# A convolution and feed-forward kernel: block products summed on VectorE, one-pass gates, separate tiles for block 1, and dummy matmuls in the opening

## Chip, cores and metric

The kernel runs on one core of one Trainium2 chip. The metric is the device time of one execution in microseconds; "before" is the kernel without the change. TensorE multiplies matrices into PSUM, VectorE and ScalarE do the element work, GpSimd (POOL) does small operations and issues one of the two busy DMA queues, SyncE (SP) issues the other.

## The reference

Four layers act on one sequence of 2048 tokens and 576 channels: a gated long convolution, a feed-forward layer, and both once more with the same weights. Cut to what matters:

```python
def _A_ref(q, k, v, shift_k, ssm_k, ssm_D):
    k_shift = sum over t in 0..3 of k_pad[:, t:t + S, :] * shift_k[:, 3 - t]   # a causal filter of 4 taps
    kv = k_shift * v
    y = irfft2(rfft2(kv padded to 2 S) * rfft2(ssm_k padded to 2 S))[:S]       # causal convolution, per channel
    y = y + kv * ssm_D
    return q * y

def _B_ref(x, w_gate, w_up, w_down):
    return (_gelu(x @ w_gate) * (x @ w_up)) @ w_down                           # 576 -> 4608 -> 576

x = A_q
x = x + _A_ref(_layernorm(x), A_k, A_v, A_shift_k, A_ssm_k, A_ssm_D)
x = x + _B_ref(_layernorm(x), B_w_gate, B_w_up, B_w_down)
x = x + _A_ref(_layernorm(x), ...)
x = x + _B_ref(_layernorm(x), ...)
```

The convolution y does not depend on x, so it is computed once and used in both A layers.

## The kernel before, in words

**Units and visits.** The tokens are cut into four chunks of 512. A unit is one feed-forward layer on one chunk, with the gate and the layernorm ahead of it; there are eight, in the order (0,0), (0,1), (1,0), (1,1), (0,2), (0,3), (1,2), (1,3) of (layer, chunk). The 4608 hidden channels are cut into three phases. A visit is one phase of one unit: twelve groups of 18 matmuls for gate and up (`gu`, L835, two halves of 64 rows side by side), a gelu on ScalarE (L1290) and a product on VectorE (L1291) for each group, and then 96 matmuls down (`down`, L1302) whose sums VectorE adds to `x_c` (L1336; L1331 in the last phase of the first layer, which also gives the sum of each row; L1322 into `ob` for the output). Units run in passes [0], [1,2], [3,4], [5,6], [7], phase by phase, so that there are 24 visits. I count them from the first.

**The convolution** (class `Conv`) works on blocks of 512 tokens, which are the chunks. For block m, `step(m)` makes queues of work: the causal filter and product on VectorE (`kv_ops`, L250, L255, L260); forward transforms of the filter's tokens `ht` and of kv on TensorE (`fwd_eo`, L281), copied out by ScalarE (L284) and crossed by VectorE (`cross`, L289, 16 operations a set), spilled to DRAM (Hd, Kd) by POOL (L336) and read again (`load`, L394, L398); products of block a with filter block m-a for each of four frequency tiles `kt` and two parts (`prod`, L298 to L302, into a bf16 tile `sum`); their addition over a by matmuls with the identity into PSUM (`accumulate`, L308), copied out by ScalarE (L491) or combined by VectorE (`both`, L316); the shift of the last block's result (`shifted`, L321); and the inverse transform on TensorE (`inverse`, L331), copied to `y` by ScalarE (L333). Blocks 1 to 3 run this way beside the visits; block 0 is in the opening.

**What sets the order.** Instructions run in program order on each engine. `Pace` keeps one estimated time for TensorE, VectorE and ScalarE, from the costs at the file's head (C_GU and so on), and `fill` puts work of the convolution and of the next unit's preparation between the groups and the down matmuls when its estimated inputs are due: `conv.run_v` for VectorE, `run_vq` for gates and norms, `run_aq` for ScalarE, `run_p` for TensorE. POOL's small operations, spills and output stores (L339) wait in `conv.spills` until due. The estimates only set the order; semaphores set the times.

**Gates and norms.** Each of 28 row tiles behind the opening gets `(x + nm) * y` (L733) and `t * rstd + x` (L740) on VectorE, the second with the sum of each row. POOL makes the negative mean (L697), ScalarE the sum of squares (L705), POOL `rstd` (L712, L713), VectorE the normed tile `xn` (L762, and a copy L764), and SP two DMA transposes into `xnT` (L792).

**The opening.** A small planner (`Plan`) lists tasks with costs and dependencies and writes out a static order: sine tables, the four taps, kv of block 0 with sums by identity matmuls (L1007), the filter turned by matmuls (L1035), the forward transforms of filter and kv (L272), products, pair sums and differences (L1097), inverses (L1110), the gates (L1144, L1155), norms, transposes (L1196), and the first three groups in two halves (`gu_half`). Block 1's filter tokens go into the one `v` buffer (tag "v"), so v of block 1 is loaded only after their transform.

Of the kernel before, what the change touches and what calls it, by code (L numbers as in the profile page):

```python
# [18 lines left out]
P = 128  # L19
# [4 lines left out]
HW = 288  # L24
# [9 lines left out]
N_KC, N_SM = 4, 6  # L34
C_TT, C_ST, C_BN, C_NORM, C_HT, C_GELU, C_EVA, C_EVD = 0.76, 0.82, 0.47, 0.62, 0.69, 0.6, 0.66, 0.76
# [33 lines left out]
class Plan:  # L69


    LAG = 0.12
# [57 lines left out]
class Conv:  # L130
# [9 lines left out]
    def __init__(self, tc, ctx, pace, A_k, A_v, A_shift_k, A_ssm_k, A_ssm_D, ident, cps, ypool):  # L140
# [15 lines left out]
        self.smp = pool("c_sm", N_SM)  # L156
# [16 lines left out]
        self.ps_free = 0.0  # L173
        self.pr_free = [0.0] * N_SM
# [3 lines left out]
        self.npr = self.nkr = self.nhr = 0  # L178
# [7 lines left out]
    def ps(self):  # L186
        return self.cps()
# [47 lines left out]
    def load_ht(self, b, eng):  # L235
        h = self.kvp.tile([P, RT, self.D], BF16, tag="v", name="ht")
        eng.dma_start(out=h[:], in_=self.hs[b].rearrange("(p i) d -> p i d", i=RT))
        self.ht[b] = h

    def kv_ops(self, b):  # L240
# [4 lines left out]
        def mult(i0, j, dst):  # L245
            def run():
                if j >= KS - 2:
# [6 lines left out]
        def add():  # L254
            nc.vector.tensor_tensor(out=st["acc"][:], in0=st["acc"][:], in1=st["tmp"][:], op=ALU.add)  # L255

        def fin(i0):
            def run():
                v = self.vt_[b]
                nc.vector.tensor_tensor(out=v[:, i0:i0 + 2, :], in0=st["acc"][:], in1=v[:, i0:i0 + 2, :], op=ALU.mult)  # L260
            return run
        for i0 in range(0, RT, 2):
            ops.append(("k", mult(i0, KS - 1, "acc")))
            for j in range(KS - 2, -1, -1):
                ops += [("k", mult(i0, j, "tmp")), ("k", add)]
            ops.append(("v", fin(i0)))
        return ops

    def fwd_full(self, ps, src, kt, s):
        for i in range(RT):  # L270
            for h in range(2):
                self.nc.tensor.matmul(ps[:, h, 0:HW], lhsT=self.fw(kt, s, i),  # L272
                                      rhs=src[:, i, h * HW:(h + 1) * HW], start=(i == 0), stop=(i == RT - 1))

    def fwd_eo(self, src, kt, s, h, scale=1.0):
# [3 lines left out]
        for e in range(2):  # L279
            for i in (e, e + 2):  # L280
                nc.tensor.matmul(ps[:, e, 0:HW], lhsT=self.fw(kt, s, i),  # L281
                                 rhs=src[:, i, h * HW:(h + 1) * HW], start=(i == e), stop=(i == e + 2))
# [8 lines left out]
    def prod(self, part, K, H, dst=None):  # L291
        nc = self.nc
        pr = self.prp.tile([P, 2, self.D], BF16, tag="prod", name="prod")
        if dst is None:
            dst = self.smp.tile([P, self.D], BF16, tag="sum", name="sum")[:]
            self.npr += 1
# [8 lines left out]
    def accumulate(self, ps, pr, first, last):  # L305
        nc = self.nc
        for h in range(2):
            nc.tensor.matmul(ps[:, h, 0:HW], lhsT=self.ident[:], rhs=pr[:, h * HW:(h + 1) * HW],  # L308
                             start=first, stop=last)

    def both(self, kt, part, first, second):

        b = {}
        for sg, op in ((0, ALU.add), (1, ALU.subtract)):
            b[sg] = self.ybp.tile([P, self.D], BF16, tag="yb", name="yb")
            self.nc.vector.tensor_tensor(out=self.halves(b[sg][:]), in0=first, in1=second, op=op)  # L316
# [28 lines left out]
    def step(self, m, kv=None, loaded=False):  # L345
# [21 lines left out]
        if loaded:  # L367
            at["k"] = at["h"] = 0.0
# [3 lines left out]
        self.L.append((lambda: self.hf_at.get(m, NEVER), lv))  # L372
# [1018 lines left out]
```

## Time and profile before

| what | us |
|---|---|
| median of 3 runs (lowest, highest) | 994.07 (993.47, 995.79) |
| the profiled execution | 996.55 |
| its span, first to last instruction | 994.8 |
| mean granted TensorE clock | 0.982 of full speed |

In a profile line, a group of instructions stands as line, engine, operation, output <- input, shape and count, then busy time, mean ns of one, and the idle time of the engine ahead of them with what ended it. PE is TensorE's matmuls and PEld its weight loads, DVE is VectorE, ACT is ScalarE, and SPq and POOLq are the DMA queues' issues. A line of stretches gives the bounds, the length, and for each engine the busy time and count; the three last numbers are TensorE's granted clock, the share of the DMA engines and GB/s. A line of waits gives who waited for whom, the total, how often, and the longest. A line of the time order gives start, length, engine, operation and, in brackets, the idle time ahead and its releaser.

### The profile page before, as it was taken

How to read it: one execution, taken by the hardware profiler on the slowest of the kernel's cores; microseconds unless marked ns; L12 is line 12 of the kernel's file. 1: busy time of each engine (PE TensorE's matmuls, PEld its weight loads, DVE VectorE, ACT ScalarE, POOL GpSimd, SP SyncE). 2: the span in 40 equal slices, each digit the busy share in tenths (PEclk: the TensorE clock that was granted, in tenths of full speed). 3: DMA queues.
4: the chain of work that ended last, by engine and by line, in shares of the span. 5: the costliest groups of instructions: out<-in, count | busy, mean ns of one | idle time of the engine just before them, and what ended most of it. 6: DMA issues, size and time to landing. Idle time of an engine off the chain costs nothing.

```text
span 994.8 us, 19408 instructions
## 1 busy us (share of the span) xinstructions
PE 957.0 (96%) x8282; PEld 551.7 (55%) x8282; DVE 547.0 (55%) x1011; ACT 299.6 (30%) x542; POOL 144.1 (14%) x308
## 2 busy tenths in 40 slices
PE   8799999599999999979999999989999999999998
PEld 5555465346646546545565565555664565466455
DVE  7756787666767565648564664465333324623322
ACT  5543412441322325304212412233112112411211
POOL 3313100512111103222010300131000000200000
PEclk9889999799999999989999999999999999999999
DMA  9979887535943721783391570374271270298730
GB/s 233 278 203 240 196 251 144 119 85 171 192 163 103 142 72 37 133 273 72 97 231 44 127 170 22 66 144 98 50 148 41 48 167 1 48 239 147 165 84 25
DMA packets 129577, 131.03 MB, mean 132 GB/s; under 512 B 43985, under 2 KB 121681, under 8 KB 129490
## 3 DMA queue, kind: packets, MB, share of 16 engines
q1 hardware_dynamic: 119554, 93.34, 43.6%
q0 software_dynamic: 9200, 35.54, 11.0%
q8 instruction: 65, 1.06, 0.5%
q10 hardware_dynamic: 736, 0.90, 0.4%
q14 instruction: 22, 0.18, 0.1%
HBM read 108.53 MB, written 11.80 MB: 121 GB/s over the span
## 4 chain that ended last, share of the span: by engine, by line
PE 89%; DVE 3%; DMA 3%; issue 2%; POOL 1%; ACT 1%; SPq 0%; POOLq 0%; DVEq 0%; ACTq 0%
PE gu L835 55%; PE dn L1302 25%; PE cps L281 2%; PE cps L308 2%; PE ps L272 2%; DMA Hd<-hh 1%; PE cps L331 1%; PE ps L835 1%; DMA wgu<-in_B_w_up_dram 1%; DMA out_dram<-ob 1%; PE ps L1007 1%; POOL rstd L713 0%; DVE hh L289 0%; DVE g_t L733 0%; DVE x_c L740 0%
## 5 line engine op out<-in xcount | busy, mean ns | idle before, releaser
L835 PE MATMUL gu<-xnT,wgu 64*128 64x512 bf16 x5130 | 568.5, 379 | 16.1 <-DVE ob L1322 6.6
L835 PEld LDWEIGHTS <-wgu 64*128 64x128 bf16 x5238 | 257.3, 95 | 328.0 <-issue 39.5
L1291 DVE TENSOR_TENSOR hT<-ga,gu 128x512 bf16<-128x512 f32 x285 | 195.8, 687 | 295.3 <-ACT ga L1290 294.3
L1290 ACT ACTIVATE ga<-gu 128x512 f32<-128x512 f32 x285 | 170.2, 597 | 575.8 <-PE gu L835 574.5
L1302 PE MATMUL dn<-wd,hT 128*128 128x288 bf16 x2304 | 299.2, 286 | 0.5 <-DVE ob L1311 0.5
L1302 PEld LDWEIGHTS <-hT 128*128 128x128 bf16 x2304 | 223.5, 98 | 66.1 <-issue 10.5
L1336 DVE TENSOR_TENSOR x_c<-x_c,dn 128x576 f32<-128x576 f32 x64 | 48.2, 753 | 62.8 <-PE dn L1302 62.2
L697 POOL TENSOR_SCALAR nm<-s 128x1 f32<-128x1 f32 x56 | 20.8, 372 | 337.1 <-DVE x_c L1331 249.8
L705 ACT ACTIVATE junk<-x_c,nm 128x576 bf16<-128x576 f32 x44 | 33.8, 768 | 18.4 <-POOL nm L697 18.4
L284 ACT ACTIVATE eo<-cps 128x576 f32<-128x576 f32 x48 | 31.2, 650 | 19.7 <-PE cps L281 14.0
L713 POOL TENSOR_TENSOR rstd<-ve,neghalf_t 128x1 f32<-128x1 f32 x56 | 35.0, 626 | 4.7
L398 POOL DMA_DIRECT2D hr<-Hd x36 | 19.5, 542 | 108.4 <-DVE prod L301 107.5
L302 DVE TENSOR_TENSOR sum<-prod 128x576 bf16<-128x576 bf16 x72 | 33.0, 458 | 2.7
L1322 DVE TENSOR_TENSOR ob<-x_c,dn 128x576 bf16<-128x576 f32 x15 | 11.3, 754 | 36.9 <-DMA out_dram<-ob 18.8
L308 PE MATMUL cps<-sum,ident 128*128 128x288 bf16 x144 | 25.2, 287 | 0.0
L394 POOL DMA_DIRECT2D kr<-Kd x24 | 13.3, 554 | 76.9 <-DVE prod L301 71.1
L712 POOL TENSOR_SCALAR ve<-ss 128x1 f32<-128x1 f32 x56 | 15.7, 281 | 44.4 <-ACT junk L705 44.4
L281 PEld LDWEIGHTS <-T 128*128 128x128 bf16 x144 | 13.5, 99 | 13.1 <-issue 9.9
L281 PE MATMUL cps<-ht,T 128*128 128x288 bf16 x72 | 15.2, 294 | 5.3 <-ACT eo L284 5.2
L289 DVE TENSOR_TENSOR hh<-eo 128x288 bf16<-128x288 f32 x48 | 19.6, 452 | 1.1 <-ACT eo L284 1.0
L289 DVE TENSOR_TENSOR kc<-eo 128x288 bf16<-128x288 f32 x48 | 19.6, 452 | 0.9 <-ACT eo L284 0.8
L301 DVE TENSOR_TENSOR prod<-kr,hr 128x576 bf16<-128x576 bf16 x48 | 19.7, 452 | 0.0
(133 smaller groups left out, 506.9 us busy)
## 6 DMA issues: line engine op xcount, KB each, us to landing
wgu<-in_B_w_gate_dram SPq DMA_DIRECT2D x45, 576.0 KB, 5.8
wd<-in_B_w_down_dram SPq DMA_DIRECT2D x30, 864.0 KB, 6.7
wgu<-in_B_w_up_dram SPq DMA_DIRECT2D x45, 512.0 KB, 7.7
hr<-Hd POOLq DMA_DIRECT2D x36, 288.0 KB, 6.4
kr<-Kd POOLq DMA_DIRECT2D x24, 288.0 KB, 5.5
Kd<-kc POOLq DMA_DIRECT2D x12, 288.0 KB, 4.9
Hd<-hh POOLq DMA_DIRECT2D x12, 288.0 KB, 5.3
k<-in_A_k_dram POOLq DMA_DIRECT2D x3, 1008.0 KB, 9.6
```

The costliest lines, as they stand in the source:

```text
L281: nc.tensor.matmul(ps[:, e, 0:HW], lhsT=self.fw(kt, s, i), rhs=src[:, i, h * HW:(h + 1) * HW], start=(i == e), stop=(i == e + 2))
L284: nc.scalar.activation(out=eo[:], in_=ps[:, :, 0:HW], func=ACT.Copy, scale=scale)
L289: self.nc.vector.tensor_tensor(out=dst, in0=eo[:, 0, :], in1=eo[:, 1, :], op=op)
L302: nc.vector.tensor_tensor(out=dst, in0=pr[:, 0, :], in1=pr[:, 1, :], op=ALU.subtract if part == 0 else ALU.add)
L308: nc.tensor.matmul(ps[:, h, 0:HW], lhsT=self.ident[:], rhs=pr[:, h * HW:(h + 1) * HW], start=first, stop=last)
L705: nc.scalar.activation(out=junk[:], in_=get_x(), func=ACT.Square, bias=v["nm"][:, 0:1], accum_out=v["ss"][:])
L713: nc.gpsimd.tensor_tensor(out=v["rstd"][:], in0=ve[:], in1=neghalf_t[:, 0:1], op=ALU.pow)
L835: nc.tensor.matmul(cols(pair[:, s, :]), lhsT=w[r0:r0 + HK, k, gi * P:(gi + 1) * P], rhs=cols(xnT[r0:r0 + HK, blk_of[k], :]), start=(k == 0 ...
L1290: nc.scalar.activation(out=ga[:], in_=pair[:, 0, :], func=ACT.Gelu_apprx_tanh)
L1291: nc.vector.tensor_tensor(out=hT[:, fi, :], in0=ga[:], in1=pair[:, 1, :], op=ALU.mult)
L1302: nc.tensor.matmul(acc[:, h, 0:HW], lhsT=hT[:, fi, j * P:(j + 1) * P], rhs=wd[2 * wb + fi // WT][:, fi % WT, h * HW:(h + 1) * HW], start=( ...
L1336: nc.vector.tensor_tensor(out=xh, in0=xh, in1=acc[:, :, 0:HW], op=ALU.add)
```

## The change

- `accumulate` and its tile pool are gone. For each `kt` and part, the first product (a = 0) is written as f32 into a tile `ac` (three buffers); each later one is added to it by VectorE (`more`). `both` reads two f32 tiles in SBUF; the order of the products changes with it, and the copy by ScalarE (L491) is gone.
- The convolution may use a second PSUM buffer, out of the rotation of the visits, while down matmuls run (`conv.alt`, `cur`).
- The gate is one pass: with m the mean, x + (x - m) * rstd * y = (x - m) * (1 + rstd * y) + m. ScalarE makes `yh = 1 + rstd * y` (one buffer), VectorE `(x + nm) * yh` with the row sum. The missing m, which the norm doesn't see, is added with the first down result of the unit (`shift`); the means have a tile of their own for that. Tasks of ScalarE get priorities, and `pressing` holds the convolution's VectorE work back when the next unit's is due.
- Block 1's filter tokens go into two buffers of the pool `hr`, and v of block 1 is loaded in the opening. The due time of reads behind a filter's store (`hd_at`) is 10 instead of 2.
- Opening: the direct term is added to one row of the turned filter on VectorE instead of to `hn` on POOL; means are made on VectorE; 9 transposes and two copies become 10 and one; 14 times 4 dummy matmuls (`busy`) follow the inverses; the inverses wait for all forward transforms; costs and priorities are changed.

```diff
-    def accumulate(self, ps, pr, first, last):
-        nc = self.nc
-        for h in range(2):
-            nc.tensor.matmul(ps[:, h, 0:HW], lhsT=self.ident[:], rhs=pr[:, h * HW:(h + 1) * HW],
-                             start=first, stop=last)
...
+                if a == 0:
+                    acc[kt, part] = self.acp.tile([P, D], F32, tag="ac", name="ac")
+                prs[part] = self.prod(part, K, hr[(kt, a)][1], acc[kt, part][:] if a == 0 else None)
...
+        def more(kt, part):
+            def run():
+                into = acc[kt, part][:]
+                nc.vector.tensor_tensor(out=into, in0=into, in1=prs[part], op=ALU.add)
+                return lambda when: None
+            return run
...
+        for kt in KTS:
+            order = [(a, part) for a in range(m + 1) for part in range(2)]
+            for a, part in order if kt < 2 else sorted(order, key=lambda k: k[1]):
                 keys = [("ld", kt, a)] + ([("kc", kt % 2, s, h) for s in range(2) for h in range(2)] if a == m else [])
-                self.V.append((lambda g=get(*keys): max(g(), self.pr_slot()), C_PR, v(kt, a, part)))
+                self.V.append((get(*keys), C_P1 if part else C_P0, v(kt, a, part)))
+                if a > 0:
+                    self.V.append((now, C_AC, more(kt, part)))
+                if kt >= 2 and a == m:
+                    self.V.append((now, 2 * C_EVD, both(kt, part)))
+                    self.V.append((now, 2 * C_TB, shift(kt - 2, part)))
...
-        if max(ready(), self.ps_free) > t.pe:
+        self.cur = 0 if self.ps_free[0] <= t.pe else 1
+        if ready() > t.pe or self.ps_free[self.cur] > t.pe or self.cur and self.alt is None:
             return False
...
-                            self.hd_at[m] = when + 2.0
+                            self.hd_at[m] = when + 10.0
...
+            nc.scalar.activation(out=g["yh"][:], in_=conv.y[c][:, j, :], func=ACT.Identity, scale=g["rstd"][:, 0:1], bias=1.0)
...
+            nc.vector.scalar_tensor_tensor(out=x_c[c][:, j, :], in0=(x_c if second else x_b)[c][:, j, :],
+                                           scalar=g["nm"][:, 0:1], in1=g["yh"][:], op0=ALU.add, op1=ALU.mult,
+                                           accum_out=v["s"][:])
+            shift[c, j] = (g["nm"], ALU.subtract)
...
+                elif ph == 0:
+                    m_, op = shift.pop((c, j))
+                    nc.vector.scalar_tensor_tensor(out=xh, in0=acc[:, :, 0:HW], scalar=m_[:, 0:1], in1=xh, op0=op, op1=ALU.add)
...
-                            hT[b] = conv.ht[b] = conv.kvp.tile([P, RT, D], BF16, tag="v", name="ht")
+                            pairs1.append(conv.hrp.tile([P, 2, D], BF16, tag="hr", name="ht"))
+                            hT[1] = conv.ht[1] = lambda i: pairs1[i // 2][:, i % 2, :]
...
+            add("POOL", 0.6, lambda: conv.load_v(1, nc.gpsimd), [x for m in KTS for x in K0[m]], prio=-20.0)
...
-                    steps.append(later(lambda me: add("PE", 0.5, me(part_of), [pA[0, m], pA[1, m], vneg], bank=(n == 0),
-                                                      prio=4.0)))
+                    steps.append(later(lambda me: add("PE", 0.5, me(part_of), [pA[0, m], pA[1, m], vneg] + H0[3] + K0[3],
+                                                      bank=(n == 0), prio=4.0 if i else 0.0)))
...
+            def busy():
+                for _ in range(4):
+                    nc.tensor.matmul(held["y", 1][:, 1, 384:512], lhsT=ident[:], rhs=ident[:], start=True, stop=True)
+            chain([add("PE", 0.22, busy, [inv[1], inv[3]], frees=[opened[1]], prio=-100.0) for _ in range(14)])
```

More of the change, by code (lines that the diff above doesn't have):

```diff
@@ L627, in ssm_geglu_kernel @@
     gwork = pool("gwork", 1)
+    gates = deque()
+    means, used = persist.tile([P, 2 * NU * RT], F32, name="means"), []
     wpool = pool("wgu", 3)
@@ L746, in act_early @@
+    shift = {}
     def act_early(c):
```

332 lines of the change are left out of this document (164 added, 168 removed).

## The prediction

> **What bounds the kernel now.** I read the page first, for the share of each engine and the chain that ended last.
>
> ```profile
> span 994.8 us, 19408 instructions
> PE 957.0 (96%) x8282; PEld 551.7 (55%) x8282; DVE 547.0 (55%) x1011; ACT 299.6 (30%) x542; POOL 144.1 (14%) x308
> PEclk9889999799999999989999999999999999999999
> PE 89%; DVE 3%; DMA 3%; issue 2%; POOL 1%; ACT 1%; SPq 0%; POOLq 0%; DVEq 0%; ACTq 0%
> ```
>
> TensorE is 89% of the chain, so the time is what TensorE must do plus the places where it stands still. What it must do is read from the chain in order of time: early groups of 18 gate/up matmuls with four others between them, and one undisturbed visit late in the run.
>
> ```profile
> 63.10 2.05 PE gu L835 x18
> 65.75 2.05 PE gu L835 x18
> 708.42 23.42 PE gu L835 x216
> 731.84 11.87 PE dn L1302 x96
> ```
>
> A visit is 23.42 + 11.87 = 35.3 us. A 128x288 matmul costs 11.87 / 96 = 0.124 us in a stream (a record is longer than that, but overlaps the next). Eighteen gate/up matmuls cost 23.42 / 12 = 1.95, four others 0.49, together 2.44; the two starts lie 2.65 apart. So each interruption of the gate/up stream costs 0.2 us more.
>
> Where it stands still: TensorE's own waits, then the stretches around the three largest (TensorE's busy time is the second number, its granted clock the third from the end).
>
> ```profile
> PE gu L835 <- DVE ob L1322: 6.6, 2, 5.2
> PE gu L835 <- issue: 6.3, 1, 6.3
> PE cps L281 <- ACT eo L284: 5.2, 6, 2.1
> PE ps L1196 <- ACT y L1149: 3.6, 1, 3.6
> PE gu L835 <- DVE x_c L1331: 2.5, 1, 2.5
> ```
>
> ```profile
> 182.00:191.00 9.00, 4.06 (x21) 2.12 (x19) 8.27 (x21) 5.35 (x11) 7.41 (x14) 0.83 0.59 116
> 191.00:197.50 6.50, 0.20 (x1) 0.01 (x1) 1.10 (x3) 0.65 (x1) 0.84 (x1) 0.50 1.07 218
> 430.50:441.40 10.90, 4.29 (x37) 1.88 (x37) 4.31 (x7) 1.19 (x2) 2.74 (x5) 0.96 1.05 373
> 441.40:455.00 13.60, 13.58 (x100) 6.29 (x101) 11.07 (x21) 5.25 (x11) 4.31 (x10) 0.78 0.11 37
> 668.50:671.60 3.10, 0.39 (x2) 0.15 (x3) 1.43 (x4) 0.76 (x2) 1.84 (x6) 1.00 0.48 95
> 671.60:685.00 13.40, 13.40 (x110) 6.80 (x112) 7.62 (x15) 5.25 (x12) 2.88 (x8) 0.87 0.58 111
> ```
>
> The reader is to see three holes, A (182 to 197.5), B (430.5 to 441.4) and C (668.5 to 671.6), and a slow clock behind B and C. B costs 6.6 of waiting and (1 - 0.78) x 13.6 = 3.0 of clock, 9.6 in all; C costs 3.1 and 0.13 x 13.4 = 1.7, 4.8.
>
> **The change part by part.** The sum is made against the profiled execution: 996.55 us, that is its span of 994.8 and 1.75 around it. It lies 2.48 above the median of the runs shown, 994.07.
>
> *Term 1, the identity matmuls.* All 144 (L308) go, and VectorE gets 48 additions of a product into an f32 tile.
>
> ```profile
> L308 PE MATMUL cps<-sum,ident 128*128 128x288 bf16 x144 | 25.2, 287 | 0.0
> L302 DVE TENSOR_TENSOR sum<-prod 128x576 bf16<-128x576 bf16 x72 | 33.0, 458 | 2.7
> L1336 DVE TENSOR_TENSOR x_c<-x_c,dn 128x576 f32<-128x576 f32 x64 | 48.2, 753 | 62.8 <-PE dn L1302 62.2
> L740 DVE SCALAR_TENSOR_TENSOR x_c<-g_t,rstd,x_c 128x576 f32<-128x576 f32 x16 | 13.0, 815 | 0.3
> L705 ACT ACTIVATE junk<-x_c,nm 128x576 bf16<-128x576 f32 x44 | 33.8, 768 | 18.4 <-POOL nm L697 18.4
> ```
>
> They had no idle time ahead of them (0.0) and stood in the stream: 144 x 0.124 = 17.8 us off TensorE. In the changed instruction order, the block-1 forwards move out of the gate/up stream of the second visit into the down stream of the first, and with the sums gone the stream is interrupted 8 times instead of 23: 15 x 0.2 = 3.0. Term 1 is 20.8.
>
> The additions cost VectorE 48 x 0.753 = 36.1 (nearest row L1336; ends 0.458 and 0.815, L302 and L740). The 24 first products of a sum now end in f32, at 0.458 or 0.753. I take 0.753, as each f32 tensor operation of this size shows: 24 x 0.295 = 7.1. The one-pass gate drops one operation of 0.815 in each of 28 gates (seven units of four), 22.8, and ScalarE gets one of about 0.77 (L705), which its 30% hide. VectorE ends near 547 + 36 + 7 - 23 = 567, or 59% of a shorter span. What counts is the tightest place: block 1, whose sums must end before its inverse.
>
> ```profile
> 96.00:139.50 43.50, 43.50 (x363) 22.99 (x362) 32.63 (x65) 13.46 (x22) 5.90 (x11) 1.00 0.90 227
> 139.50:165.70 26.20, 26.20 (x231) 10.98 (x230) 21.44 (x38) 7.73 (x13) 0.00 (x0) 1.00 0.72 176
> ```
>
> There VectorE was busy 54.1 us in the second visit and the gate/up part of the third. The 16 crosses (6.6, at 0.41 apart like the pair of L1097 below) move into the first visit; 8 additions (6.0) and 8 dearer products (2.4) come: 55.9. The time for it, up to the inverse after 26 down matmuls, is 35.3 + 23.4 + 3.2 = 61.9. It fits by 6 us, so I cost the additions at 1 us of TensorE's waiting (0 to 8: without the cover, the 8.4 are TensorE's).
>
> The Trainium skill, "VectorE: DVE Perf Modes", section "What auto-detection actually checks", says the fast two-source mode needs every tensor in 16 bits. The kernel's own cost list (C_P0, C_P1) books the first products as if the f32 result kept it. By the skill's rule VectorE falls 2.4 us behind the plan in block 1, inside the 6; by the cost list it does not. The rows of before have no bf16 pair with an f32 result, so none decides it.
>
> *Term 2, the opening.*
>
> ```profile
> 36.59 0.76 DVE L298 TENSOR_TENSOR prod<-kc,h 128x1152 bf16<-128x1152 bf16 x1 [3.40 <-ACT h L1058]
> 38.99 0.82 DVE L1097 TENSOR_TENSOR yb<-yb 128x576 bf16<-128x576 bf16 x2
> 39.73 1.53 DVE L1144 SCALAR_TENSOR_TENSOR x_c<-x_b,mv,ps 128x576 f32<-128x576 bf16 x2
> 49.74 4.02 PE L835 MATMUL ps<-xnT,wgu 64*128 64x256 bf16 x36 [2.07 <-ACT xnT L1202]
> 57.98 1.16 PE L835 MATMUL ps<-xnT,wgu 64*128 64x256 bf16 x18 [1.24 <-ACT xnT L1202]
> 40.00:50.00 10.00, 4.32 (x39) 3.52 (x38) 8.59 (x20) 6.43 (x13) 4.21 (x10) 0.73 1.08 254
> ```
>
> The last product waited for a filter transform (3.40). In the changed order, the 24 inverse matmuls that stood ahead of those transforms come behind them: 24 x 0.124 = 3.0 earlier. Five sums and differences instead of two stand in VectorE's queue ahead of the first gate: 3 x 0.41 = 1.2 later. From there to the first transposes one gate operation (0.81) goes and the mean is no longer taken on POOL; one ScalarE operation (about 0.77) and two of one column on VectorE come. I take 0.9 gained, an estimate between 0 and 2 from these two. The 36 half matmuls took 4.02 at a clock near 0.73; at full clock they take 2 x 0.97 = 1.95, and 56 dummy matmuls now stand in the hole ahead of them: 2.1. From 57.98 on, the other halves follow sooner, as both late transposes stand ahead of the third half: about 1.2. Sum 6.0. Ends: 2 (the clock alone) and 8 (all waits up to 62 gone). Block 1's v comes in the opening too, 576 KB or 2.3 us at the 254 GB/s of the last row; its first reader is over 30 us later.
>
> *Term 3, stall A.*
>
> ```profile
> 165.73 6.30 PE L1302 MATMUL dn<-wd,hT 128*128 128x288 bf16 x50
> 171.86 1.14 PE L331 MATMUL cps<-yb,V 128*128 128x288 bf16 x8
> 188.90 0.57 DVE L762 TENSOR_SCALAR xn<-x_c,nm,rstd 128x576 bf16<-128x576 f32 x1
> 185.05 9.10 SPq L792 DMA_TRANSPOSE xnT<-xn  x6
> ```
>
> The down matmuls of the third visit began at 165.7 and the next visit at 197.5, 31.8 later. The inverse moves from 50 down matmuls to 26, so one expects the hole to close. But in VectorE's changed order the last two norms (L762) still stand behind the add of the visit's last down result and behind the crosses of block 2, and the transposes then go one after another, 9.1 us for six. Those ends are tied to the down stream, not to the inverse. I take 31.0, a gain of 0.8 (ends: loss 2, gain 11 if the inverse sets it).
>
> *Term 4, stall B.*
>
> ```profile
> 420.58 1.07 POOL L336 DMA_DIRECT2D Hd<-hh  x2 [0.56 <-DVE hh L289]
> 432.96 0.55 POOL L398 DMA_DIRECT2D hr<-Hd  x1 [0.43 <-DMA Hd<-hh]
> 433.76 0.55 POOL L339 DMA_DIRECT2D out_dram<-ob  x1 [0.25 <-issue]
> 440.61 0.75 DVE L1322 TENSOR_TENSOR ob<-x_c,dn 128x576 bf16<-128x576 f32 x1 [3.74 <-DMA out_dram<-ob]
> ```
>
> An output store waited in POOL's queue behind reads of Hd, which waited for Hd's own store; so ob and its PSUM bank came free late. Now block 3's filter is stored a visit earlier, and the due time of such reads is 10 us behind the store instead of 2. Only two loads stand between the four stores of that visit, and they wait for a product, not a store. Gain 9.0 of 9.6 (ends 0 and 9.6).
>
> *Term 5, stall C.* By the instruction order it was the fourth chunk's inverse, split over the two visits just ahead of its first reader. In the changed order it stands two visits earlier: gain 4.8 (ends 0 and 4.8).
>
> The fused shift (L1336 becomes a form like L1331) stays near 0.75 us; the separate mean tiles cost nothing, as no instruction is added by them.
>
> Sum: 20.8 - 1 + 6.0 + 0.8 + 9.0 + 4.8 = 40.4. 994.8 - 40.4 = 954.4 span, 956.2 for such an execution, 953.7 as a median.
>
> **The rivals.**
> - *The early inverse closes A.* If the four norms follow the inverse and not the last add, A gives 11 instead of 0.8: 943.5. For it: the inverse comes 24 down matmuls earlier. Against: the queue order above. 0.13.
> - *VectorE becomes late.* If TensorE waits for block 1's 8.4 us of new work and half of block 2's (16 additions and 8 dearer products, 14.4): 953.7 + 15.6, about 969. For it: 90% of 61.9 us is taken. Against: 6 us free. 0.10.
> - *The change doesn't do what it says for B and C:* stores still queue behind loads, and the stall stays under another name: 953.7 + 9 to 13.8, about 965. 0.09.
> - *The dummies don't hold the clock.* The first 36 halves stay at 4.02: 955.8. The Trainium skill, "TensorE: Matmul & The Clock Gate", "Part 1: The HAM clock gate", gives 3.4 us of activity as the measure of its gate; by its rule a hole of the 3.6 us waited at L1196 halves the clock, and one below it does not. The trace agrees: 0.73 from 40 to 50. 0.06, inside the forecast's range.
> - *Slower.* VectorE sets the pace of blocks 1 and 2. They hold 56 f32 operations (24 additions, 16 first products, 16 pair operations). To eat 40.4 + 2 us each must cost 0.76 more than 0.753, so 1.5 us; it decides from there. The dearest row of that size is 0.815. 0.04.
>
> **How the numbers follow.** Forecast 0.58 with the range 945 to 962; the rivals as given, and the clock case among them. The range 942 to 970 takes in the opening's ends (-2, +4), A's, and the late cases, and leaves out the slower rival and a sum of mishaps. A measurement here can tell about 0.2%, 2 us, from no change. Faster 0.94, same 0.02, slower 0.04.
>
> **What would show it.** No matmul with the identity inside the visits; about 8200 matmuls, 56 of them dummies; gate/up stretches of 23.4 us in one piece from the second visit on; first gate/up halves near 46 and the clock at 1.00 there; the additions at 0.75 us with TensorE never waiting for yb; a hole of some 10 us still ahead of the fourth visit; no wait for ob near 400. I am wrong if TensorE waits for VectorE's sums, if the hole ahead of the fourth visit is gone, or if POOL's loads again hold the stores.

## The result and the profile after

The changed kernel takes 961.26 us (median of 4 runs, 960.22 to 961.29), the kernel before 993.77 on the same chip (4 runs, 992.29 to 995.79): a ratio of 0.9669, 95% interval 0.965 to 0.9688. It is 32.5 us faster and lies inside the range, 7.6 us above the forecast of 953.7. The profiled execution took 961.26, span 959.5; against the span of before, 35.3 us are gone where 40.4 were summed. So 5.1 of the 7.6 us are in the terms. The other 2.5 are the step from a profiled execution to the median, which was 2.48 for before and nothing here.

The page of the changed kernel: span, busy time of each engine, granted clock, and the shares of the chain that ended last.

```profile
span 959.5 us, 19259 instructions
...
PE 931.6 (97%) x8198; PEld 540.0 (56%) x8198; DVE 562.7 (59%) x1030; ACT 312.8 (33%) x560; POOL 139.0 (14%) x302
...
PEclk9999999799999999999999999999999999999999
...
PE 92%; DMA 2%; issue 2%; DVE 1%; ACT 1%; POOL 0%; SPq 0%; DVEq 0%; ACTq 0%; POOLq 0%
```

TensorE went from 89% to 92% of the chain. Of the clock row's slow slices one is left, the eighth, 168 to 192 us: stall A. TensorE's waits say the same; these are the ones that matter here (what waited, for what, us in total, times, longest).

```profile
PE gu L837 <- DMA xnT<-xn: 7.4, 1, 7.4
PE cps L285 <- ACT eo L288: 5.2, 3, 2.5
...
PE cps L285 <- DVE x_c L1359: 1.4, 2, 0.7
...
PE gu L837 <- DVE ob L1350: 1.0, 1, 1.0
...
PE cps L285 <- DVE x_c L1365: 0.8, 2, 0.7
...
PE cps L285 <- DVE ob L1350: 0.6, 1, 0.6
```

The wait of 6.6 for ob is down to 1.0, and no wait for yb is in the list. New are the waits of cps for x_c and ob: block matmuls that use a down result's PSUM bank wait for the operation that reads it. The chain in order of time shows the visits (start, us, line, matmuls).

```profile
95.76 23.42 PE gu L837 x216
...
131.04 23.42 PE gu L837 x216
154.46 3.29 PE dn L1330 x26
...
187.08 25.87 PE gu L837 x216
```

The gate/up parts are in one piece from the second visit on. From the third visit's first down matmul to the fourth visit lie still 32.7 us. The opening ends 4.65 earlier: the first whole gate/up group starts at 58.39 instead of 63.04. That is one pair of executions: over the nine traces with this opening (after and eight of the runs) that group starts at 57.2 to 58.4, over the three with the old one at 61.8 to 64.5, and the means lie 5.3 apart.

Set against the forecast's terms, by the lengths of the visits in the two traces (us of span, gains positive):

| term | forecast | measured | from |
|---|---|---|---|
| 1 identity matmuls | 17.8 | 17.6 | 144 x 0.122 (a down part with 14 of them took 13.58, one without 11.87) |
| 1 interruptions | 3.0 | 3.1 | second and third gate/up part: 30.70 and 26.19, less 23.42 and their 42 and 14 other matmuls |
| 1 additions on VectorE | -1 | 0 | no wait for yb |
| 2 opening | 6.0 | 4.65 | 63.04 to 58.39 |
| 3 stall A | 0.8 | -1.2 | 31.79 to 32.69, and the visit behind it 25.50 to 25.81 |
| 4 stall B | 9.0 | 9.9 | gate/up part of 33.33 to 23.42 |
| 5 stall C | 4.8 | 5.1 | 2.6 in the down part and 2.5 in the visit behind it, gone |
| not foreseen: waits for a second PSUM bank | 0 | -2.7 | four down parts 0.4 to 1.3 longer than their matmuls, less 0.7 by which before's were |
| not foreseen: a wait for ob late in the run | 0 | -1.2 | one gate/up part of 24.59 |
| sum | 40.4 | 35.3 | |

The prediction weighed two prices for VectorE's first products, and one row settles it. These are VectorE's groups by shape (mean ns behind the comma).

```profile
L476 DVE TENSOR_TENSOR ac<-ac,prod 128x576 f32<-128x576 f32 x48 | 36.2, 754 | 0.7
L305 DVE TENSOR_TENSOR prod<-prod 128x576 bf16<-128x576 bf16 x48 | 22.0, 458 | 1.7
...
L305 DVE TENSOR_TENSOR ac<-prod 128x576 f32<-128x576 bf16 x24 | 18.2, 758 | 0.8
```

The same line costs 0.458 with a bf16 result and 0.758 with an f32 result. The kernel's own cost list is wrong here. The trace agrees with the rule of the Trainium skill that the prediction cites, "VectorE: DVE Perf Modes", "What auto-detection actually checks".

### The profile page after: what moved, and what is told of

It reads as the page before. It is cut to its first block, busy times and chain, and to the rows that moved or that the text cites. A ratio compares the mean times of both kernels' runs of the same rounds, so it can differ in the third digit from the quotient of the medians.

```text
span 959.5 us, 19259 instructions
## 1 busy us (share of the span) xinstructions
PE 931.6 (97%) x8198; PEld 540.0 (56%) x8198; DVE 562.7 (59%) x1030; ACT 312.8 (33%) x560; POOL 139.0 (14%) x302
## 4 chain that ended last, share of the span: by engine, by line
PE 92%; DMA 2%; issue 2%; DVE 1%; ACT 1%; POOL 0%; SPq 0%; DVEq 0%; ACTq 0%; POOLq 0%
PE gu L837 57%; PE dn L1330 27%; PE cps L285 2%; PE ps L276 2%; PE cps L328 1%; DMA out_dram<-ob 1%; DMA xnT<-xn 1%; PE ps L837 1%; DMA k<-in_A_k_dram 1%; PE ps L1015 1%; PE ps L1121 1%; PE ps L1047 0%; PE ps L1142 0%; ACT yh L731 0%; DVE x_c L741 0%
## 5 line engine op out<-in xcount | busy, mean ns | idle before, releaser
L837 PE MATMUL gu<-xnT,wgu 64*128 64x512 bf16 x5130 | 561.2, 377 | 8.4 <-DMA xnT<-xn 7.4
L1330 PE MATMUL dn<-wd,hT 128*128 128x288 bf16 x2304 | 292.8, 286 | 0.5 <-DVE ob L1339 0.5
L1367 DVE TENSOR_TENSOR x_c<-x_c,dn 128x576 f32<-128x576 f32 x32 | 24.1, 753 | 39.1 <-PE dn L1330 38.9
L692 POOL TENSOR_SCALAR means<-s 128x1 f32<-128x1 f32 x28 | 9.4, 336 | 227.7 <-DVE x_c L1359 193.8
L1365 DVE SCALAR_TENSOR_TENSOR x_c<-dn,means,x_c 128x576 f32<-128x576 f32 x28 | 22.8, 815 | 24.8 <-PE dn L1330 24.8
L476 DVE TENSOR_TENSOR ac<-ac,prod 128x576 f32<-128x576 f32 x48 | 36.2, 754 | 0.7
L391 POOL DMA_DIRECT2D kr<-Kd x24 | 13.3, 552 | 100.3 <-DVE prod L304 100.3
L731 ACT ACTIVATE yh<-y,rstd 128x576 f32<-128x576 bf16 x28 | 21.6, 772 | 14.0 <-DVE x_c L741 11.5
L305 DVE TENSOR_TENSOR prod<-prod 128x576 bf16<-128x576 bf16 x48 | 22.0, 458 | 1.7
L1359 DVE SCALAR_TENSOR_TENSOR x_c<-dn,x_c 128x576 f32<-128x576 f32 x16 | 12.1, 757 | 17.5 <-PE dn L1330 16.6
L700 ACT ACTIVATE junk<-x_c,nm 128x576 bf16<-128x576 f32 x28 | 21.5, 768 | 1.3 <-POOL nm L692 1.3
```

Of the source, the lines that this page charges most:

```text
L305: nc.vector.tensor_tensor(out=dst, in0=pr[:, 0, :], in1=pr[:, 1, :], op=ALU.subtract if part == 0 else ALU.add)
L476: nc.vector.tensor_tensor(out=into, in0=into, in1=prs[part], op=ALU.add)
L731: nc.scalar.activation(out=g["yh"][:], in_=conv.y[c][:, j, :], func=ACT.Identity, scale=g["rstd"][:, 0:1], bias=1.0)
L837: nc.tensor.matmul(cols(pair[:, s, :]), lhsT=w[r0:r0 + HK, k, gi * P:(gi + 1) * P], rhs=cols(xnT[r0:r0 + HK, blk_of[k], :]), start=(k == 0 ...
L1330: nc.tensor.matmul(acc[:, h, 0:HW], lhsT=hT[:, fi, j * P:(j + 1) * P], rhs=wd[2 * wb + fi // WT][:, fi % WT, h * HW:(h + 1) * HW], start=( ...
L1365: nc.vector.scalar_tensor_tensor(out=xh, in0=acc[:, :, 0:HW], scalar=m_[:, 0:1], in1=xh, op0=op, op1=ALU.add)
```

## The experiments

A ratio is against the kernel before on the same chip; a length of a visit is from the kernel's own trace. The opening's start moves by up to 1.4 us from one execution to the next, as its first loads land earlier or later, so for small effects I compare lengths from the first whole gate/up group to the start of the last visit: 892.3 us in before, 861.6 in after. Stall A moves too. With the gate/up part behind it, it is 58.5 us long in after and 57.3 to 57.7 in three kernels whose edits leave it alone (a_add2x, a_nodummy, a_dummy40), so a gain on A that is taken against after can be up to 1.2 us too large.

### Term 1: what an identity matmul costs

```
     def accumulate(self, ps, pr, first, last):
-        for h in range(2):
+        for again in range(2):
+            for h in range(2):
                 (start only in the first round, stop only in the second)
```

*b_ident2x*: The kernel before, with the sums' matmuls doubled.

> The kernel before with each of its 144 identity matmuls issued twice into the same sum, so the sums hold every product twice and the output is not the reference's; nothing else is changed, the plan neither. Theory (term 1: each costs TensorE 0.124 us in the stream and none is hidden in a wait): 144 x 0.124 = 17.8 us slower, about 1012, each visit longer by 0.124 for every identity matmul that it holds. Rival (part of them stands in TensorE's waits, so that removing them gave less than 17.8): 5 to 12 us slower.

1011.85 us, ratio 1.0165 (1.0142 to 1.0189), 16.4 us slower. The group of the doubled matmuls, with the idle time ahead of them in the last column:

```profile
L309 PE MATMUL cps<-sum,ident 128*128 128x288 bf16 x288 | 42.9, 286 | 0.0
```

The down part with 14 of them went from 13.58 to 15.30, 0.123 each; so the price per matmul is right. From the first group to the last visit the kernel is 14.6 longer, not 17.6: stalls A, B and C shrank by 0.5, 1.6 and 0.9, so they took in part of the work that was put ahead of them. The theory holds for the price. That the whole 17.6 counts in after, where B and C are gone, follows from the lengths of the visits; no run tested it by itself.

### Term 1: has VectorE room for the additions?

```
         def more(kt, part):
...
+                nc.vector.tensor_tensor(out=into, in0=into, in1=prs[part], op=ALU.add)
                 nc.vector.tensor_tensor(out=into, in0=into, in1=prs[part], op=ALU.add)
```

*a_add2x*: The changed kernel, with the additions doubled.

> The changed kernel with each of VectorE's 48 additions into the f32 sums issued twice (36 us more of VectorE, 6.0 of them in block 1, 12 in block 2, 18 in block 3), so a product is added twice and the output is not the reference's; the plan doesn't know of it. Theory (VectorE has 6 to 7 us free in block 1 and more behind it): 0 to 3 us slower. Rival (the sums set TensorE's pace already): 6 + 12 = 18 us slower, TensorE waiting for yb.

967.18 us, ratio 0.9716 (0.9699 to 0.9733); from the first group to the last visit 5.65 longer than after. Busy time by stretches, first the changed kernel, then this one; the rows are block 1's second and third gate/up parts with the down part between, and the three visits of block 3's heaviest sums.

```profile
95.70:154.40 58.70, 58.70 (x530) 30.18 (x529) 51.80 (x91) 13.75 (x23) 5.35 (x10) 1.00 0.93 240
...
456.20:550.20 94.00, 94.00 (x842) 49.93 (x841) 80.12 (x139) 26.60 (x51) 14.07 (x27) 1.00 0.55 136
```

```profile
95.30:154.25 58.95, 58.88 (x529) 30.19 (x529) 56.08 (x98) 13.74 (x23) 5.33 (x10) 1.00 0.89 228
...
458.20:555.60 97.40, 95.04 (x842) 53.03 (x842) 94.99 (x162) 26.73 (x51) 13.50 (x28) 1.00 0.54 131
```

VectorE's busy time is the third of the busy columns. In block 1 it had 6.9 us free (51.80 of 58.70), took the extra work, and the stretch grew by 0.25. In block 3 it went from 80 of 94 to 95 of 97 us, and the time grew by 3.4; block 2's fifth, seventh and eighth visits grew by 3.0 in all, and stall A was 0.8 shorter. So the rival, by which VectorE sets the pace already, is refuted (18 forecast); the theory's 0 to 3 was too low, since the room in block 3 is 14 us, less than the 18 put in. The change as made costs TensorE nothing here.

### Term 4: what removed stall B

```
-                            self.hd_at[m] = when + 2.0
+                            self.hd_at[m] = when + 10.0
```

*b_due10*: The kernel before, with the later due time alone.

> The kernel before with one number changed: the due time of the reads of a block's own filter transforms (hd_at) is 10 us behind their store instead of 2. In the order of POOL's queue this moves three of the four output stores of the stalled visit ahead of nine loads, and nothing else behind that visit. Theory (stall B is output stores standing behind loads that wait for a store): the visit that took 33.33 us for its gate/up part takes 23.4, and the time falls by 9.5 us (8 to 10.5), to about 984.3. Rival (ob and its bank come free late for another reason, the loads only stand beside it): no change, 993.8.

990.1 us, ratio 0.9954 (0.9937 to 0.997): 4.6 us faster (3.0 to 6.3). The stalled gate/up part is down from 33.33 to 26.58, that is 6.75 of the 9.9, where the theory had 9.5; from the first group to the last visit the trace is 6.35 shorter. What is left of it, from the timeline of this kernel (the brackets give the wait and what ended it):

```profile
421.22 0.62 POOL L232 DMA_DIRECT2D v<-in_A_v_dram  x1 [10.48 <-PE cps L281]
...
422.39 1.07 POOL L336 DMA_DIRECT2D Hd<-hh  x2 [0.56 <-DVE hh L289]
...
424.70 0.54 POOL L339 DMA_DIRECT2D out_dram<-ob  x1 [1.23 <-DVE ob L1322]
...
435.14 0.76 DVE L1322 TENSOR_TENSOR ob<-x_c,dn 128x576 bf16<-128x576 f32 x1 [7.80 <-DMA out_dram<-ob]
```

No read stands among the stores any more, and yet the first output store, issued at 424.70 right behind a load of v and two stores of Hd, landed 10.3 us later, and ob waited 7.80 for it. So the first cause of B is shown, stores behind reads that wait (6.75 us). The rest I put down to a store behind 1.1 MB of other transfers; that is read from this timeline, and no run moved those transfers alone. The same store took 10.3 us in before too.

The other half of the question is whether the changed kernel needs the later due time.

```
-                            self.hd_at[m] = when + 10.0
+                            self.hd_at[m] = when + 2.0
```

*a_due2*: The changed kernel, with the earlier due time.

> The changed kernel with the due time put back to 2 us. The plan then also puts block 1's inverse ahead of the first down matmul of the third visit instead of behind 26, and spreads block 2's filter transforms otherwise. Theory: stall B stays away, because in the changed kernel block 3's filter transforms are stored a visit ahead of their readers; and stall A stays, because the late norms hang on the down results: time within 2 us of 961.3. Rival 1 (the due time alone removed B): 9 to 10 us slower, about 971. Rival 2 (the inverse sets stall A): the inverse comes 3.2 us earlier and so does the fourth visit, about 958.

964.94 us, ratio 0.9697 (0.9676 to 0.9719); from the first group to the last visit 2.1 longer than after. Stall B did not come back (its gate/up part took 23.42), so in the changed kernel the due time is not what removes it, and rival 1 is refuted. What is left is the earlier place of block 3's transforms, which no run moved by itself. The median lies 3.7 us above after, more than the 2 that were expected. The loss is elsewhere: the plan spread block 1's forward transforms otherwise, the first visit's down part took 21.28 us instead of 16.20, and the matmuls that left stall A came back as 1.0 us in the part ahead of it and 2.6 in the next down part. Stall A got shorter by 7.1 us with the visit behind it (32.69 + 25.81 to 23.34 + 28.03), 2.5 of it because 20 block matmuls moved out; the section on A comes back to it.

### Term 2: the dummies

```
-            chain([add("PE", 0.22, busy, ...) for _ in range(14)])
```

*a_nodummy*: The changed kernel without dummies.

> The changed kernel without the 56 dummy matmuls and without the copy's wait for them. The prediction's step: the first 36 half matmuls take 4.0 us again instead of 2.14, the rest of the opening keeps its times: 1.9 to 2.1 us slower, about 963.3. Theory now, from the trace of after: the dummies also stood ahead of the first transposes of xn, which began 44.93 though their xn was done at 43.4; without them the transposes come about 1.4 us earlier, so only 0.5 us slower, 961.8. Rival (the clock recovers without dummies): 1.4 us faster, 959.9.

```
-            chain([add("PE", 0.22, busy, ...) for _ in range(14)])
+            chain([add("PE", 0.22, busy, ...) for _ in range(10)])
```

*a_dummy40*: The changed kernel with 40 of them.

> The changed kernel with 10 groups of dummies (40 matmuls) instead of 14 (56): the four ahead of the first transposes, which waited 0.9 us, and the twelve ahead of the second ones go. Theory (those dummies held the transposes back, and the 40 are enough for the clock): first half matmuls 1.0 to 1.4 us earlier at 2.14 us for 36, time about 960.1. Rival 1 (the transposes wait for something else): no change, 961.3. Rival 2 (the last 16 hold the clock): the 36 halves take up to 4.0 us, up to 1.9 us slower less what the transposes gain.

959.43 us without dummies (ratio 0.9642, 0.9625 to 0.9658) and 959.37 with 40 (0.9642, 0.9625 to 0.966); after's interval (0.965 to 0.9688) overlaps both, so the times alone don't part them. Both are near 959.9, the time of a_nodummy's rival, by which the clock recovers without dummies, but that is luck: from the first group to the last visit the two traces are 2.35 and 1.97 shorter than after, all of it in stall A and in the late wait for ob, which the edits don't touch. The timelines of the opening part them. The changed kernel, from its last product of the opening on:

```profile
33.53 0.76 DVE L301 TENSOR_TENSOR prod<-kc,h 128x1152 bf16<-128x1152 bf16 x1 [0.33 <-ACT kc L1088]
...
44.71 0.38 PE L1142 MATMUL ps<-ident 128*128 128x128 bf16 x4 [0.91 <-ACT yh L1162]
...
44.93 0.39 PE L1217 MATMUL ps<-ident,xn 128*128 128x128 bf16 x4
...
48.16 2.14 PE L837 MATMUL ps<-xnT,wgu 64*128 64x256 bf16 x36 [0.94 <-DVE xnT L1222]
...
58.39 1.90 PE L837 MATMUL gu<-xnT,wgu 64*128 64x512 bf16 x16
```

Without dummies:

```profile
31.95 0.76 DVE L301 TENSOR_TENSOR prod<-kc,h 128x1152 bf16<-128x1152 bf16 x1 [0.33 <-ACT kc L1088]
...
41.90 0.40 PE L1216 MATMUL ps<-ident,xn 128*128 128x128 bf16 x4 [1.91 <-DVE xn L1202]
...
45.22 3.68 PE L837 MATMUL ps<-xnT,wgu 64*128 64x256 bf16 x36 [0.94 <-DVE xnT L1221]
...
56.98 2.12 PE L837 MATMUL gu<-xnT,wgu 64*128 64x512 bf16 x18
```

From the last product to the first transposes of xn: 11.40 us with dummies, 9.95 without, since four dummies waited for ScalarE's yh ahead of the transposes in TensorE's queue. The 36 half matmuls then take 2.14 instead of 3.68. To the first whole group it is 24.86 against 25.03: the dummies give 1.54 us and take 1.45. With 40 of them the transposes came early, but the halves took 3.81 and the way was 25.44. So the clock did not recover without dummies, the last 16 hold it, rival 2 of the run with 40 is right, and that run's theory (40 are enough) falls.

### Term 3: what sets the end of stall A

The changed kernel's timeline around A, in VectorE, POOL, SP's queue and TensorE:

```profile
165.20 0.57 POOL L708 TENSOR_TENSOR rstd<-ve,neghalf_t 128x1 f32<-128x1 f32 x1
...
169.25 0.76 DVE L1359 SCALAR_TENSOR_TENSOR x_c<-dn,x_c 128x576 f32<-128x576 f32 x1 [4.00 <-PE dn L1330]
...
169.93 0.82 DVE L741 SCALAR_TENSOR_TENSOR x_c<-x_b,means,yh 128x576 f32<-128x576 bf16 x1
...
170.67 0.58 DVE L770 TENSOR_SCALAR xn<-x_c,nm,rstd 128x576 bf16<-128x576 f32 x1
...
171.49 11.59 SPq L798 DMA_TRANSPOSE xnT<-xn  x8
...
180.18 0.60 POOL L648 DMA_DIRECT2D x_b<-in_A_q_dram  x1
...
187.08 1.52 PE L837 MATMUL gu<-xnT,wgu 64*128 64x512 bf16 x6 [7.44 <-DMA xnT<-xn]
```

The first norm (L770, 170.67) had its rstd at 165.8, but stood in VectorE's queue behind the third gate and the third down add, which waited 4.00 for TensorE. The prediction named the late norms, the adds and the crosses; the first run takes block 2's evictions and crosses away.

```
-  self.Pq.append((lambda: max(get("h")(), NEVER if self.neo > 1 else 0.0), 0.49, fwd_h(kt, s, h)))
+  self.Pq.append((lambda: max(get("h")(), NEVER if self.neo > 1 else 0.0, self.hold(m)), 0.49, fwd_h(kt, s, h)))
+  conv.hold = lambda m: NEVER if m == 2 and xn_done.get(1, 0) < RT else 0.0
```

*a_hold*: The changed kernel, with block 2's filter transforms held back.

> The changed kernel with block 2's filter transforms (32 matmuls, their evictions and crosses) held back until the four tiles of unit 1's xn are on their way, that is behind stall A: 24 matmuls (3.0 us) leave the third visit's down part, and no eviction or cross stands ahead of the late norms. The inverse stays behind 26 down matmuls. Theory (the late norms hang on the down results and the crosses): the fourth visit starts 5 us earlier, of which 3.0 come back later as TensorE's own work, so 2 us faster (1 to 4) than after. Rival (the inverse sets the end of stall A): the fourth visit starts no earlier, and the 3.0 us of work come on top: 3 us slower.

960.31 us, ratio 0.9646 (0.963 to 0.9663); from the first group to the last visit 861.7 against 861.6. The fourth visit starts 29.15 after the third's first down matmul instead of 32.69, 3.5 earlier, of which 3.0 is the work moved out; the rest is within what A differs by between traces. The moved matmuls made the next down part 3.9 longer, 1.0 of it more than their own work, so the kernel gained nothing. Neither theory nor rival: the crosses were not the price, and the inverse is not the end either. The last norm now started 19.7 us after that matmul instead of 24.0, and TensorE still waited 13.3:

```profile
168.68 10.85 SPq L798 DMA_TRANSPOSE xnT<-xn  x8
...
177.37 0.61 POOL L648 DMA_DIRECT2D x_b<-in_A_q_dram  x1
...
183.29 2.31 PE L838 MATMUL gu<-xnT,wgu 64*128 64x512 bf16 x10 [13.29 <-DMA xnT<-xn]
```

The eight transposes go back to back here, 10.85 / 8 = 1.36 us with small gaps. So a new theory: SP's queue sets the end, counted from the first norm.

```
-        lag = 2 if layer == 0 else 1
+        lag = 2 if layer == 0 and ui != 1 else 1
```

*a_hold_lag1*: The same, with the norms of unit 1 one gate earlier.

> As a_hold, and in unit 1 each norm stands one gate behind its own gate in VectorE's queue instead of two, so that the first norm no longer stands behind the third gate and the add ahead of it. Theory, new after a_hold (SP's queue sets the end of stall A: eight DMA transposes go one after another at 1.25 us from the first norm on, 168.7 to 179.5 in a_hold, and the last lands 3.8 later): the first norm comes 2 us earlier, the fourth visit starts 27.0 us after the third visit's first down matmul instead of 29.15, 958.2. Rival (the last norm sets it): 29.1 again, 960.3.

956.64 us, ratio 0.9605 (0.9587 to 0.9623). The fourth visit starts after 23.78 us, 5.4 earlier than in a_hold and 3.2 earlier than I expected; its gate/up part then takes 26.85 instead of 25.66, so 4.2 are kept. The timeline, and then how long the transposes took from issue to landing:

```profile
165.38 0.58 DVE L770 TENSOR_SCALAR xn<-x_c,nm,rstd 128x576 bf16<-128x576 f32 x1 [0.56 <-POOL rstd L708]
...
166.21 11.45 SPq L798 DMA_TRANSPOSE xnT<-xn  x8
...
177.75 0.61 PE L838 MATMUL gu<-xnT,wgu 64*128 64x512 bf16 x2 [7.92 <-DMA xnT<-xn]
...
177.81 0.60 POOL L648 DMA_DIRECT2D x_b<-in_A_q_dram  x1
...
178.92 7.40 PE L838 MATMUL gu<-xnT,wgu 64*128 64x512 bf16 x44 [0.56 <-DMA xnT<-xn]
```

```profile
DMA to landing us min/median/max: 2.5/2.6/2.7
```

In the changed kernel that row reads 2.5/2.6/7.1. The transposes were issued 2.3 us earlier in the visit, as the theory has it (from 14.54 us after the first down matmul to 12.24), their series took 0.6 longer, and the other 3.7 come from the landing of the seventh, which fell from 6.3 to 2.6. (The trace has no landing for the eighth; TensorE used it 2.5 us after its issue.) What differs is the 576 KB load of the next unit's x (L648), in a_hold the one other transfer issued in that stretch ahead of the last transpose. Over eleven kernels with eight such transposes the largest landing goes with it: where that load was issued ahead of the last transpose (before, after and seven of the runs) it was 6.2 to 7.2, and where it came behind, 2.7. The second kernel of that kind besides a_hold_lag1 is a_due2, where the load came 0.37 us behind the eighth's issue, and there the row hides a landing:

```profile
183.00 0.61 PE L837 MATMUL gu<-xnT,wgu 64*128 64x512 bf16 x2 [6.16 <-DMA xnT<-xn]
...
186.28 4.09 PE L837 MATMUL gu<-xnT,wgu 64*128 64x512 bf16 x21 [2.67 <-DMA xnT<-xn]
```

The first two matmuls need the first half of every tile, the third needs the second halves, and the last of those, issued at 181.59, was used only 4.7 us later. So a_due2 met the load with its eighth transpose. Of the 7.1 us by which its A is shorter, the seventh's earlier issue gave 4.9 and its landing 4.5, and the visit behind lost 2.2 again. The Trainium skill, "DMA: Bandwidth & Descriptors", "Issuing engines are not separate DMA queues", says that transfers of all issuing engines run on the same 16 DMA engines and interleave; these landings agree. The load alone was not moved in any run, and in eight of the nine two stores of 288 KB stand beside it, so the collision is shown by the runs side by side, not isolated.

The third way is to take the transposes off the DMA.

```
-            spread(xnT_of[ui], j, xn)
+            (turn_xn1 if ui == 1 and j >= 2 else spread)(xnT_of[ui], j, xn)
     # turn_xn1: ten small transposes into the block's PSUM bank, then nc.scalar.copy into xnT
```

*a_turn*: The changed kernel, with two tiles turned by TensorE.

> The changed kernel with the last two of unit 1's four xn tiles turned by TensorE (20 small matmuls into a PSUM bank and one copy by ScalarE each) instead of by DMA; the norms keep their places. Theory (from the last norm, done at 179.1 in after, to the fourth visit at 187.1 lie 1.3 of SP's queue and 7.1 of landing, and nothing else): TensorE's turn and the copy take about 2.2 us, the fourth visit starts 5.7 us earlier, 955.6. Rival 1 (the first two tiles' DMA transposes or a load end as late): 0 to 2 us faster. Rival 2 (the norms themselves slip, as ScalarE's queue gets the copies): no gain.

956.58 us, ratio 0.9613 (0.9594 to 0.9633); the fourth visit starts after 29.28 us and runs 24.89, 4.3 better than after where 5.7 were expected (3.1 to 3.5 against the three other traces of A). The turn waited 2.5 for a block 2 eviction of the same bank, and the second tile 1.2 for the first one's copy.

*a_turn_hold_lag1*: The three edits on stall A together.

> a_turn, a_hold and the shorter distance of unit 1's norms together. Theory: with four DMA transposes only and no block 2 eviction or cross ahead, the last norm (20.3 us after the third visit's first down matmul in a_hold), its turn on TensorE and the copy end near 23.1; a_turn had 29.3 with 20 forwards (2.5 us) more in it, so 3.7 faster than a_turn, about 953. Rival (ScalarE's copies or the first tiles' transposes end later): 25 to 26, about 955.5.

955.51 us, ratio 0.96 (0.9584 to 0.9616); the fourth visit starts after 25.41, in the rival's range, and 1.6 later than with DMA transposes that meet no load. The visit behind gives that back: start and gate/up part together are 50.7 us, and 50.6 in a_hold_lag1. ScalarE's queue is why the start comes late:

```profile
176.92 0.77 ACT L731 ACTIVATE yh<-y,rstd 128x576 f32<-128x576 bf16 x1 [0.89 <-DVE x_c L741]
...
177.60 1.10 ACT L810 COPY xnT<-xt 128x1152 bf16<-128x1152 bf16 x1
```

The last tile was turned by 175.7, but its copy stood behind two gate factors of a later unit, the second of which waited for VectorE.

### The second PSUM bank, and all parts together

```
-                conv.alt = lambda: pr("cps")
+                conv.alt = (lambda: pr("cps")) if ui == 0 else None
```

*a_onebank3*: The changed kernel, with the second bank in unit 0's visits only.

> The changed kernel with the second PSUM bank for block work given out only in unit 0's visits. Theory (from the fifth visit on, the matmuls that use a down result's bank wait for the addition that reads it: 0.9 to 1.2 us in each of the visits V4, V7 and V8): these down parts take 15.8 us instead of 16.7 to 17.05, 2.6 faster, 958.7. Rival (the block work that then comes later makes TensorE wait elsewhere): 961 or more.

957.39 us, ratio 0.9614 (0.9598 to 0.9631). The fifth visit's down part went from 16.69 to 15.78, the ninth's from 17.05 to 15.93, and the seventh's and eighth's together from 32.49 to 31.57: 2.95 in all, where 2.6 were expected. The theory holds; the measured time fell by more. The rest is stall A, 1.2 shorter in this execution, which is what A differs by between traces without any edit to it.

*a_all3*: The last two together.

> a_turn_hold_lag1 and a_onebank3 together. Theory (the parts lie in different visits and add up): 953 - 2.6, about 950.5. Rival (block 3's plan shifts by a visit, and stores stand behind loads again): a wait for ob of some us, 955 or more.

953.14 us, ratio 0.9574 (0.956 to 0.9589), 41.8 us faster than before and the best of the kernels run. No new wait for ob came; the late one of after is still there (0.9). It falls short of 950.5, as a_turn_hold_lag1 did of its own 953. The same with DMA transposes, a_hold_lag1 with the single bank, was not run; by the lengths above (50.6 and 50.7) it should be no faster.

## Why the prediction was right, and where it missed

- **The bound was read right.** TensorE's work and its three holes set the time. The tight terms came from rows of the same shape: 0.124 a matmul (0.122 measured, and 0.123 when doubled), 0.2 an interruption (3.1 of 3.0).
- **VectorE in block 1: right, with the 1 us not needed.** 55.9 of 61.9 us were forecast busy; 51.80 of 58.70 are, to the end of the third gate/up part. The f32 products cost 0.758, as taken. The fused shift, taken at 0.75, takes 0.815, 28 times, 1.8 us of VectorE's time in all.
- **The opening: 4.65 of 6.0.** The last product came 3.06 earlier (3.0 forecast; so near a match is luck, as it is 32.3 to 33.5 in the traces with this opening and 36.3 to 37.9 in the old one), the halves ran at the full clock (1.9 of 2.1) and the other halves followed 1.2 sooner (1.2). From the product to the first gate 1.85 were lost instead of 1.2. And the step that failed is that the dummies only fill a hole: they stood ahead of the transposes in TensorE's queue and cost 1.45 us, nearly all that the clock gave. The first halves started at 48.16; the forecast's own terms give 47.0, and its "near 46" was a slip.
- **Stall A: right that it stays, wrong about what holds it.** "Those ends are tied to the down stream" named the adds, which do hold the first norm (2.3 us by a_hold_lag1), but taking the crosses away gained nothing beyond the moved work (a_hold), and the step left out is the landing: I took the transposes' own 9.1 us as the end and did not look at what else was on the DMA when the last one landed. The rival by which the early inverse closes A is wrong for this change: the 24 down matmuls by which the inverse came forward moved nothing. In a_due2 it stands ahead of the first down matmul, 20 block matmuls are out as well, and the last norm comes 18.2 us after that matmul instead of 24.0; so the inverse is one of the things ahead of the norms, and its share is open.
- **Stall B: right in sum, and only in part in cause.** The order of POOL's queue was 6.75 of 9.9; the rest is read as a store landing behind other transfers. Of the two reasons given, the later due time is not needed in the changed kernel (a_due2), which leaves the earlier store, not tested by itself.
- **Stall C** went as forecast (5.1 of 4.8). No run put its inverse back, so the cause is argued from the order alone.
- **Missed altogether: the second PSUM bank (2.7 us).** The diff gives block work a down result's bank; I priced what the matmuls cost and not whether that bank is free. It is free only when the addition that reads it is done. The wait for ob late in the run (1.2) was 0 in a_nodummy and 0.25 in a_dummy40, where a store landed 1.2 and 0.9 us sooner, and is left open.
- **The offset of 2.48 between profile and median** was carried over as if it belonged to the kernel. It does not: here it is nothing.

## What to carry to other kernels

Ask of a stall that ends with a transfer two things: when the first transfer of its series could be issued and what stands ahead of it in the issuing engine's queues, and what else is on the DMA when the last one lands. Fill work on an engine is free only if nothing that matters stands behind it in that engine's queue. And work that gets a second buffer from another stage's rotation takes over that stage's release time too.

## What the runs showed of the hardware that was not expected

- The granted clock fell without a long wait. With 40 dummies TensorE was busy 1.21 of 2.80 us, its longest wait 0.94, and the clock of the next 3.8 us was 0.55; with 56 it was busy 2.22 of 3.10 and the clock stayed at 1.00 (us of the stretch, then TensorE's busy time; the clock is third from the end). First the kernel with 40, then the changed kernel.

```profile
43.50:46.30 2.80, 1.21 (x14) 0.78 (x14) 2.39 (x8) 2.80 (x6) 0.64 (x1) 1.00 1.11 221
46.30:50.10 3.80, 3.74 (x37) 3.04 (x37) 1.16 (x2) 1.24 (x3) 1.75 (x4) 0.55 1.10 237
```

```profile
45.00:48.10 3.10, 2.22 (x34) 1.70 (x31) 1.60 (x5) 2.43 (x5) 0.86 (x2) 1.00 0.75 292
48.10:50.30 2.20, 2.14 (x37) 1.96 (x38) 1.09 (x2) 0.93 (x3) 1.52 (x3) 1.00 1.04 401
```

  The prediction read the rule of the Trainium skill, "TensorE: Matmul & The Clock Gate", "Part 1: The HAM clock gate", as one about the length of a hole. Here no wait was longer than 0.94 us, so the length of one wait doesn't explain the fall. Two readings are left, and no run parts them: a stretch that is more than half idle in small pieces is enough, or its 14 matmuls count for less, as all of them are transposes of xn (L1215, L1217), where the other stretch holds 12 dummies as well.
- A half of a tile's DMA transpose lands 2.5 to 2.7 us after its issue, and the latest of eight took 6.2 to 7.2 where a load of 576 KB was issued ahead of the last one.
- A store of 144 KB took 10.3 us to land behind a load and two stores of 1.1 MB together.
